# Whole-row query-weight transfers, copied first columns, another order at the layer's end, and the last output-weight rows on eight DMA engines

## The chip, the cores and the metric

The kernel runs on one core of one Trainium2 chip. The metric is the device time of one execution in microseconds (us). The kernel before takes 2003.55 us (median of 4 runs, 2002.02 to 2005.01).

## The reference, cut to what matters

Four attention layers with one query token each run one after the other; layers 0 and 2 share the tensors A, layers 1 and 3 share B. Everything is bfloat16.

```python
D = 640; H = 32; Sk = 8192; Dh = 192             # k_cache, v_cache: (1, 32, 8192, 192); wq (640, 6144); wo (6144, 640)
def attn(x, k_cache, v_cache, wq, wo):
    q = (x @ wq)...                               # 32 heads of 192
    scores = einsum("bhqd,bhkd->bhqk", q, k_cache) * Dh ** -0.5
    p = softmax(scores); o = einsum("bhqk,bhkd->bhqd", p, v_cache)
    return o.reshape(...) @ wo
for W in (A, B, A, B):
    x = x + attn(layernorm(x), *W)
```

A K or V block of one head is 8192 x 192 x 2 bytes = 3072 KB. There are 256 of them in the four layers, six of which the kernel keeps on chip from a layer to the next use. Each is used once against a single query, so nearly all of the time is moving some 849 MB.

## The kernel before

PE is the engine of the matrix products (TensorE), DVE the vector engine, ACT the scalar engine; SP issues the transfers. The kernel has eight slots in SBUF (the on-chip memory of 128 partitions), each big enough for one K or V block. A plan lists all transfers in order; a transfer is issued on one queue (SP) as soon as the slot's last user is done. `m` are a head's products and score matmuls, `s` its softmax, `v` its values, `wq` and `wo` the projections.

```python
# the plan of a layer (cut and shortened)
if l == 0: plan.append(("k", 0, 0)); plan.append(("wq0", 0))
...
elif p < H - 2:  part = [("m", l, p), ("s", l, p), ("v", l, p)]
elif p == H - 2: part = [("m", l, p)]
else:            part = [("m", l, p), ("s", l, p - 1), ("s", l, p), ("v", l, p - 1), ("v", l, p)]
...
if p == H // 2 + 4 and l + 1 < NL: plan.append(("wq0", l + 1))   # next layer's first columns, early
plan.append(("wo", l, 2)); steps.append(("wo", l, 2)); plan.append(("wol", l))

# the transfers (cut and shortened): first two heads' columns of wq, rows of 768 bytes; rest of wq in three pieces of row groups
wq0[:]  <- w["wq"][:, q0:q0 + 2 * DH].rearrange("(p c) n -> p c n", c=5)
t[...]  <- w["wq"][:, q1:q1 + QC].rearrange("(p c) n -> p c n", c=5)[:, c0:c0 + k, :]
# the last two heads' rows of wo (the remainder), 480 KB, behind the third wo part in the same slot
wol     <- w["wo"][wol * DH:(wol + 2) * DH].rearrange("(p i) n -> p i n", p=128)

# a head's products: DVE multiplies K by q in four chunks, PE adds the products up with 24 matmuls
for c in range(4): DV.op(tensor_tensor(k3[:, :, d0:d0 + QD], kin[...], q_sb[...], mult))
for c in range(4): PE.wait(chunks[c]); ... matmul(S, ident, k3[...]) x6
```

Two heads' K blocks come right before their V blocks at the end of a layer: K 30, K 31, V 30, V 31, then the third wo part and the remainder. At the end of layer 1, six of the eight slots hold blocks that are kept, so only two are left to stream through.

## Time and profile before

| what | before | where read |
|---|---|---|
| time | 2003.55 us | median of 4 runs |
| DMA queue's share of 16 engines' span | 99.3% | page, part 3 |
| one K or V block | 7.31 us | distance of landings |
| spread of a block's sixteen landings, start / 1000 us / end | 0.7 / 8.1 / 8.3 us | landings in the trace |
| the stall of layers 1 to 2 | 375 GB/s in its slice | page, part 2 |
| last K, last V fully landed, end of the span | 1973.9, 1988.5, 2002.9 us | landings, page |

Lines of the page of the kernel before: the span, the DMA share in tenths and the GB/s in 40 slices of 50 us, and the DMA queues (q1 carries the kernel's own transfers, q8 and q14 instructions).

```profile
span 2002.9 us, 20412 instructions
...
DMA  9999999999999999999999999999999999999997
GB/s 404 433 430 426 431 430 426 431 431 428 425 431 429 431 429 430 426 432 428 429 375 432 430 429 431 431 427 430 429 429 428 430 428 431 431 429 429 429 431 321
DMA packets 44055, 850.65 MB, mean 425 GB/s; under 512 B 4800, under 2 KB 7360, under 8 KB 7872
...
q1 hardware_dynamic: 43824, 849.37, 99.3%
q8 instruction: 70, 1.15, 0.2%
```

The DMA engines are full nearly always, and the slices say where they are not: the first, the 21st (layer 1 to 2) and the last. Small packets stand out too: 7360 - 4800 = 2560 packets between 512 bytes and 2 KB are the four 768-byte-row transfers.

The timeline of the kernel before at its end (start us, duration us, engine, line, operation, tiles; in brackets the idle time before it and what ended that). L482 are the values' matmuls, L512 the gather of the last heads, L402 the output projection.

```profile
1986.33 2.73 PE L482 MATMUL O<-slot,p_sb 128*2 128x384 bf16 x32
...
1989.75 1.44 PE L512 MATMUL TB<-small,o_sb 128*64 128x1 f32 x12 [0.69 <-ACT o_sb L490]
1991.12 2.73 PE L482 MATMUL O<-slot,p_sb 128*2 128x384 bf16 x32
...
1995.91 3.16 PE L402 MATMUL YB<-oT,slot 128*128 128x1 bf16 x75
```

The last head's values (the second L482 line) have no wait for DMA in brackets: their block had landed at 1988.5, and they queue behind the values and the gather of the head before. The products of that head had started at 1973.93, as its K landed (1973.90).

The same view around the stall of layers 1 to 2, the last product and projection lines:

```profile
999.96 6.76 DVE L433 TENSOR_TENSOR slot<-slot,q_sb 128x3072 bf16<-128x3072 bf16 x4 [0.54 <-DMA slot<-in_B_k_cache_dram]
...
1020.31 3.16 PE L402 MATMUL YB<-oT,slot 128*128 128x1 bf16 x75 [0.22 <-DMA slot<-in_B_wo_dram]
```

Here the projection waits only for wo's landing. The stall starts after that: wq's second piece is asked for when the projection has freed wo's slot, at 1024.1 us.

### The profile page before, as it was taken

How to read it: one execution, taken by the hardware profiler on the slowest of the kernel's cores; microseconds unless marked ns; L12 is line 12 of the kernel's file. 1: busy time of each engine (PE TensorE's matmuls, PEld its weight loads, DVE VectorE, ACT ScalarE, POOL GpSimd, SP SyncE). 2: the span in 40 equal slices, each digit the busy share in tenths (PEclk: the TensorE clock that was granted, in tenths of full speed). 3: DMA queues.
4: the chain of work that ended last, by engine and by line, in shares of the span. 5: the costliest groups of instructions: out<-in, count | busy, mean ns of one | idle time of the engine just before them, and what ended most of it. 6: DMA issues, size and time to landing. Idle time of an engine off the chain costs nothing.

```text
span 2002.9 us, 20412 instructions
## 1 busy us (share of the span) xinstructions
PE 1406.5 (70%) x10438; PEld 323.9 (16%) x7494; DVE 1047.1 (52%) x1072; ACT 217.6 (11%) x657; POOL 4.6 (0%) x22
## 2 busy tenths in 40 slices
PE   5666767667667767767777676676677768767667
PEld 1111111111211111111131111111112212111112
DVE  3454554556345456455535546545564465554554
ACT  0111111111011111111101111111110111111110
POOL 0000000000000000000000000000000000000000
PEclk8788888888688798787878888888886888887887
DMA  9999999999999999999999999999999999999997
GB/s 404 433 430 426 431 430 426 431 431 428 425 431 429 431 429 430 426 432 428 429 375 432 430 429 431 431 427 430 429 429 428 430 428 431 431 429 429 429 431 321
DMA packets 44055, 850.65 MB, mean 425 GB/s; under 512 B 4800, under 2 KB 7360, under 8 KB 7872
## 3 DMA queue, kind: packets, MB, share of 16 engines
q1 hardware_dynamic: 43824, 849.37, 99.3%
q8 instruction: 70, 1.15, 0.2%
q14 instruction: 17, 0.14, 0.0%
q10 hardware_dynamic: 144, 0.00, 0.0%
HBM read 849.35 MB, written 0.00 MB: 424 GB/s over the span
## 4 chain that ended last, share of the span: by engine, by line
DMA 70%; PE 17%; DVE 12%; ACT 1%; issue 1%; another core or an unknown queue 0%; SPq 0%; DVEq 0%
DMA slot<-in_A_k_cache_dram 35%; DMA slot<-in_B_k_cache_dram 34%; PE S L58 11%; DVE slot L433 10%; PE O L482 2%; DMA slot<-in_A_wq_dram 1%; PE S L446 1%; PE TB L497 1%; DVE s_sb L453 1%; ACT p_sb L463 1%; PE TB L467 0%; PE QT L366 0%; DVE small L460 0%; PE YB L402 0%
## 5 line engine op out<-in xcount | busy, mean ns | idle before, releaser
L433 DVE TENSOR_TENSOR slot<-slot,q_sb 128x3072 bf16<-128x3072 bf16 x512 | 865.8, 1753 | 465.3 <-DMA slot<-in_A_k_cache_dram 239.5
L58 PE MATMUL S<-slot,ident 128*128 128x512 bf16 x2944 | 795.6, 424 | 34.1 <-DVE slot L433 34.1
L482 PE MATMUL O<-slot,p_sb 128*2 128x384 bf16 x4096 | 356.8, 428 | 0.0
L446 PE MATMUL S<-slot,ident 128*128 128x512 bf16 x128 | 60.9, 476 | 249.4 <-DVE slot L433 249.2
L453 DVE TENSOR_REDUCE s_sb<-S 128x64 f32<-128x512 f32 x128 | 88.4, 691 | 241.6 <-PE S L58 241.6
L482 PEld LDWEIGHTS O<-slot,p_sb 128*2 128x2 bf16 x4096 | 130.5, 88 | 138.9 <-issue 106.5
L497 PE MATMUL TB<-o_sb,small 128*1 128x192 f32 x480 | 124.0, 391 | 36.3 <-DVE small L471 28.0
L392 ACT ACTIVATE q_sb<-QM 128x192 bf16<-128x192 f32 x120 | 39.7, 331 | 970.7 <-PE QM L385 970.7
L385 PEld LDWEIGHTS QM<-ident,qT 128*128 128x128 bf16 x240 | 23.0, 98 | 731.2 <-issue 715.9
L467 PE MATMUL TB<-small,ones 128*128 128x1 f32 x256 | 50.7, 267 | 109.9 <-ACT p_sb L463 109.9
L457 PE MATMUL QM<-ident,m_bf 128*128 128x128 bf16 x128 | 27.7, 216 | 129.5 <-DVE m_bf L456 129.5
L490 ACT ACTIVATE o_sb<-O,small 128x384 f32<-128x384 f32 x128 | 74.4, 581 | 238.8 <-PE O L482 238.8
L471 DVE RECIPROCAL small<-TB 128x1 f32<-128x1 f32 x128 | 21.5, 168 | 123.3 <-PE TB L467 123.3
L463 ACT ACTIVATE p_sb<-s_sb,small 128x64 bf16<-128x64 f32 x128 | 44.5, 348 | 290.7 <-DVE small L460 290.7
L446 PEld LDWEIGHTS S<-slot,ident 128*128 128x128 bf16 x128 | 12.7, 99 | 331.3 <-DVE slot L433 330.9
L460 DVE TENSOR_REDUCE small<-QM 128x1 f32<-128x128 f32 x128 | 37.3, 291 | 53.2 <-PE QM L457 53.2
L467 PEld LDWEIGHTS TB<-small,ones 128*128 128x128 f32 x256 | 39.9, 196 | 129.6 <-ACT p_sb L463 129.6
L503 ACT ACTIVATE orow<-TB 1x192 bf16<-1x192 f32 x120 | 38.4, 320 | 205.4 <-PE TB L497 205.4
L497 PEld LDWEIGHTS TB<-o_sb,small 128*1 128x1 f32 x480 | 33.5, 89 | 77.7 <-DVE small L471 37.2
L457 PEld LDWEIGHTS QM<-ident,m_bf 128*128 128x128 bf16 x128 | 12.2, 96 | 208.1 <-ACT q_sb L392 131.6
L402 PE MATMUL YB<-oT,slot 128*128 128x1 bf16 x900 | 37.9, 178 | 3.1 <-ACT oT L417 2.2
L402 PEld LDWEIGHTS YB<-oT,slot 128*128 128x128 bf16 x900 | 36.9, 131 | 3.9 <-ACT oT L417 2.9
(47 smaller groups left out, 220.3 us busy)
## 6 DMA issues: line engine op xcount, KB each, us to landing
slot<-in_B_k_cache_dram SPq DMA_DIRECT2D x64, 3072.0 KB, 36.1
slot<-in_A_k_cache_dram SPq DMA_DIRECT2D x63, 3072.0 KB, 23.2
slot<-in_A_v_cache_dram SPq DMA_DIRECT2D x63, 3072.0 KB, 26.3
slot<-in_B_v_cache_dram SPq DMA_DIRECT2D x60, 3072.0 KB, 36.9
slot<-in_A_wo_dram SPq DMA_DIRECT2D x6, 2400.0 KB, 26.3
slot<-in_B_wo_dram SPq DMA_DIRECT2D x6, 2400.0 KB, 34.0
slot<-in_A_wq_dram SPq DMA_DIRECT2D x4, 2880.0 KB, 22.2
slot<-in_B_wq_dram SPq DMA_DIRECT2D x4, 2880.0 KB, 30.7
```

The source lines that it names most:

```text
L58: return t.add_instruction(mybir.InstMatmult(name=t.bass.get_next_instruction_name(), engine=mybir.EngineType.PE, ins=[t.lower_ap(rhs), t. ...
L392: lambda a: a.activation(q_sb[i][:], QM[:, 0:DH], ACT.Copy), e, last["q"][i], bank=use["QM"])
L402: e = PE.op(lambda t, i=i, c=c, f=y_first[0], fin=fin: t.matmul(YB[:, c:c + 1], lhsT=t3[:, i, c:D:DC], rhs=o[:, i:i + 1], start=f, stop=fi ...
L433: e = DV.op(lambda v, d0=d0: v.tensor_tensor(k3[:, :, d0:d0 + QD], kin[:, :, d0:d0 + QD], q_sb[qi][:, d0:d0 + QD].unsqueeze(1).broadcast_t ...
L446: t.matmul(S[:, :], lhsT=ident[:], rhs=k3[:, :, d0:d0 + R], start=True, stop=fin) if d0 == 0 else
L453: ev_s = DV.op(lambda v: v.tensor_reduce(s_sb[par][:], S[:].rearrange("p (j r) -> p j r", r=R), AX.X, ALU.add), ev_S[h], last["s"][par], b ...
L457: e = PE.op(lambda t: t.matmul(QM[:, C_MX:C_MX + P], lhsT=m_bf[par][:, 0:1].broadcast_to([P, P]), rhs=ident[:], start=True, stop=True), ev ...
L463: ev_p[h] = AC.op(lambda a: a.activation(p_sb[par][:], s_sb[par][:], ACT.Exp, bias=negm[par][:, 0:1], accum_out=l_col[par][:]), ev_n, ev_s ...
L467: e = PE.op(lambda t: t.matmul(TB[:, C_L + par:C_L + par + 1], lhsT=ones[:], rhs=l_col[par][:], start=True, stop=True), ev_p[h], last["L"] ...
L482: e = PE.op(lambda e, g=g, j=j, f=m < G, fin=fin: e.matmul(OB[par][32 * g:32 * g + 2, 0:2 * DH], lhsT=p_sb[par][:, j:j + 2], rhs=t[:, j * ...
L490: lambda a: a.activation(o_sb[:], OB[par][:, 0:2 * DH], ACT.Copy, scale=rl[par][:, 0:1]),
L497: e = PE.op(lambda t, i=i: t.matmul(TB[0:1, C_O:C_O + DH], lhsT=pick[:, i:i + 1], rhs=o_sb[:, i * DH:(i + 1) * DH], start=(i == 0), stop=( ...
```

## The change

Its intent: fewer bytes and no small packets (wq of layers 0 and 1 as one transfer of whole rows, 61440 bytes a partition; the first columns that layers 2 and 3 need are copied on chip); a shorter stall (wq's first piece of layer 2 is one row group instead of two, the remainder of wo has its own step and shares the next wq's slot); evened-out DMA engines (the remainder of layers 0 to 2 by eight engines); a shorter tail (another order at the layer's end, and wo's last three row groups as the last transfer). The diff, cut to its core (the two comments after # are added here):

```diff
-    Q_PARTS = [(c, min(2, DC - c)) for c in range(0, DC, 2)]
-    OI = O_LAST * DH // P
+    Q_PARTS = [[(0, 2), (2, 2), (4, 1)] if l < 2 else [(0, 1), (1, 2), (3, 2)] for l in range(NL)]
+    O_PART = [P // 2, P // 2, P // 2, P]
+    OI = [O_LAST * DH // n for n in O_PART]
+    NB = 3
...
-        slot = [sb(f"slot{i}", [P, J * DH], BF16) for i in range(NSLOT)]
+        pool = sb("pool", [P, NSLOT * TS], BF16)          # one tile, so three adjacent slots can hold a whole wq
...
-                    part = [("m", l, p), ("s", l, p - 1), ("s", l, p), ("v", l, p - 1), ("v", l, p)]
+                    part = [("s", l, p - 1), ("m", l, p), ("v", l, p - 1), ("s", l, p), ("v", l, p)]
...
             plan.append(("wol", l))
+            steps.append(("wol", l))
+        plan.append(("wob", NL - 1))
...
+                k = O_PART[l] // O_LAST
+                for h in range(O_LAST):
+                    e = SP.op(lambda s, h=h: s.dma_start(
+                        wol_rows(l)[h * k:(h + 1) * k],
+                        w["wo"][r0 + h * DH:r0 + (h + 1) * DH].rearrange("(q e i) n -> e q (i n)", e=8, i=OI[l])),
+                        *free, sem=semOL, inc=16)
...
+            elif n[0] == "wq" and l < 2:
+                f = lambda s: s.dma_start(pool[:, i * TS:i * TS + DC * QW], w["wq"].rearrange("(p c) n -> p (c n)", c=DC))
...
+                ev_first[l] = DV.op(lambda v: v.tensor_copy(wq0[l][:], whole[:, :, q0:q0 + Q_FIRST * DH]), e)
...
+                for o, i in parts:                          # o_sb of the last two heads, permuted, in two ACT operations
+                    ev_os[h] = AC.op(lambda a, o=o, i=i: a.activation(o, i, ACT.Copy, scale=rl[par][:, 0:1]), ...)
```

## The prediction

> **What bounds it.** The DMA engines. The page gives them 99.3% of the span and 9 tenths or more in nearly every slice; PE has 70%, DVE 52%. A 3072 KB K or V block lands every 7.31 us, all through the kernel. So the time is bytes per engine, plus the places where engines idle, plus the work after the last landing. The trace shows three such places.
>
> 1. *Uneven engines.* A transfer's sixteen landings lie 0.7 us apart at first and 8.1 us at 1000 us, with seven engines ahead and nine some 6 us behind. The instruction queue's 70 packets of 16 KB (about 1.06 us each, durations repeating with period eight) fit a load on half of the engines only. The last engine decides.
> 2. *Layer 1 to 2 (slices of 375 GB/s).* Six of eight slots are kept, and wq's pieces wait for slots: between 1012 and 1050 us the first engines idle about 10 us, the last about 4.
> 3. *The end.* The last product ends at 1982.2, V of the last head lands at 1988.5, but its matmuls start only at 1991.2, behind those of the head before. Then 1.44 us gather, 3.7 us projection (90 matmuls), and some 3 us to the end.
>
> **What changes.**
> - The four transfers of 768-byte rows go (36 ns a packet, 40 an engine: 1.47 us each, read from landings). Two whole-row wq transfers take in their bytes (1.14 us each): 5.9 - 2.3 = 3.6 us less on each engine.
> - Three wo remainders (480 KB) go to eight engines: 2.28 us each on those, none on the others, where it was 1.14 on all. The Trainium skill, "DMA: Bandwidth & Descriptors", "Why a DMA increments its semaphore by 16 and not by 1", says that a transfer uses the largest count of engines up to 16 that divides both sides' slowest dimension, the lowest-numbered ones: here eight. No run shows yet that those are the engines that run ahead; I assume it. Then the late ones end 3.4 us earlier.
> - Layer 2's first wq piece is one row group instead of two, its first heads' columns are already on chip, and wo's slot is released before the remainder. The first K of layer 2 should be asked for about 4 us earlier; idle falls by about 1.6 us (late engines) to 4 us (early ones).
> - At layer ends the softmax and values of head 30 come earlier, so head 31's values can start when V lands: about 2.5 us off the tail. The last three wo row groups arrive last, off the chain.
> - Costs: wq whole, 18.3 us, lands before layer 0 and 1 begin. Four or more blocks are queued behind it, so DMA should not stop. Copies of first columns (1 us of DVE, estimate) are hidden.
>
> **Sum.** Late engines' DMA end: 3.6 + 3.4 + 1.6, about 8.7 us earlier; tail about 2.3 us shorter; together 11 us of 2003.8. Predicted 1992.7 us, range 1989 to 1998. Chances: faster by over 2% 0.01, within 2% 0.97, slower by over 2% 0.02.
>
> **What would show it.** No 768-byte packets; HBM bytes 848.4 MB; spread of landings before the end about 4 us instead of 8.3; the dip at slice 21 smaller but there; chain at the end: head 31's values waiting for DMA, not for PE; last V landing near 1980.
>
> **What would make it wrong.** The eight engines being the late ones (then about 1996 to 1998); a stall at layer 0 to 1, where three adjacent slots must be free at once; long rows delaying instruction fetches or the small x load; whole wq moving slower than 27 GB/s an engine.

## The result, and the profile after

The changed kernel takes 2004.72 us (median of 4 runs: 2003.06, 2002.31, 2006.42, 2006.38); before takes 2003.55 us. The ratio is 1.0005, 95% interval 0.9988 to 1.0022: the same time. Ratios here are the mean time of one kernel's runs over that of the other's runs of the same rounds, so not quite the ratio of the medians quoted beside them.

The page of the changed kernel, the same lines:

```profile
span 2000.9 us, 20649 instructions
...
DMA  9999999999999999999999999999999999999997
GB/s 410 430 430 431 429 429 430 431 431 428 426 431 431 428 430 431 430 430 430 429 380 431 429 428 431 431 428 429 431 428 421 429 430 430 430 428 430 430 430 307
DMA packets 40296, 849.69 MB, mean 425 GB/s; under 512 B 4688, under 2 KB 4688, under 8 KB 5136
...
q1 hardware_dynamic: 40064, 848.38, 99.2%
q8 instruction: 71, 1.16, 0.2%
```

The small packets are gone (4688 under 512 B and as many under 2 KB), and 0.99 MB as well. The traced run is 2.0 us shorter than that of the kernel before, and the last slice is emptier, not fuller: DMA ends earlier, and more time passes after it.

The timeline of the changed kernel at its end. L492 are the products, L58 the score matmuls, L541 the values, L462 the projection.

```profile
1971.99 0.69 DVE L512 TENSOR_REDUCE s_sb<-S 128x64 f32<-128x512 f32 x1 [3.53 <-PE S L58]
...
1974.65 6.75 DVE L492 TENSOR_TENSOR pool<-pool,q_sb 128x3072 bf16<-128x3072 bf16 x4
...
1976.84 7.75 PE L58 MATMUL S<-pool,ident 128*128 128x512 bf16 x23
1984.53 1.47 PE L541 MATMUL O<-pool,p_sb 128*2 128x384 bf16 x32
...
1988.68 2.48 PE L541 MATMUL O<-pool,p_sb 128*2 128x384 bf16 x32
...
1993.58 2.56 PE L462 MATMUL YB<-oT,pool 128*128 128x1 bf16 x60
```

The last K block had fully landed at 1970.52 us, 3.4 us earlier than before. But its products start at 1974.65, 4.1 us after the landing: DVE first has to finish the softmax of head 30, and that waited 3.53 us for the score matmuls of head 30. The values of the last head start 3.6 us after their V block's landing (1985.13), where it had been 2.6. From the last K's landing to the end it is 30.4 us (2000.9 - 1970.5) instead of 29.0.

The landings, taken from the trace's semaphore updates (last engine, in us):

```
                        before     changed
third wo part, layer 0  512.72     509.25
third wo part, layer 1  1020.26    1017.26
second wq piece asked   1024.10    1020.50
first K after stall     1049.96    1046.82
last K                  1973.90    1970.52
last V                  1988.51    1985.13    (predicted: near 1980)
spread at the last V    8.3        7.1        (predicted: about 4)
```

So DMA gains 3.4 us on its late engines instead of the 8.7 predicted, and the tail gives back more than 1 us instead of gaining 2.3. Both errors needed an explanation, and so did the two slow runs of four, 4 us above the others. (A slow run is here one of 2006 us or more.)

### The profile page after: what moved, and what is told of

Read it like the earlier page. It is cut to its first block, busy times and chain, and to the rows that moved or that the text cites. A ratio compares the mean times of both kernels' runs of the same rounds, so it can differ in the third digit from the quotient of the medians.

```text
span 2000.9 us, 20649 instructions
## 1 busy us (share of the span) xinstructions
PE 1404.3 (70%) x10555; PEld 323.1 (16%) x7611; DVE 1049.4 (52%) x1074; ACT 219.8 (11%) x665; POOL 4.5 (0%) x22
## 2 busy tenths in 40 slices
DMA packets 40296, 849.69 MB, mean 425 GB/s; under 512 B 4688, under 2 KB 4688, under 8 KB 5136
## 4 chain that ended last, share of the span: by engine, by line
DMA 67%; PE 20%; DVE 11%; issue 1%; ACT 1%; SPq 0%; another core or an unknown queue 0%; DVEq 0%
DMA pool<-in_A_k_cache_dram 33%; DMA pool<-in_B_k_cache_dram 31%; PE S L58 13%; DVE pool L492 9%; PE O L541 2%; DMA pool<-in_B_wq_dram 1%; DMA x_bf<-in_A_x_dram 1%; DMA pool<-in_B_wo_dram 1%; PE S L505 1%; PE TB L564 1%; PE QT L424 1%; DVE s_sb L512 1%; PE YB L462 1%; ACT p_sb L522 0%; PE TB L526 0%
## 5 line engine op out<-in xcount | busy, mean ns | idle before, releaser
L492 DVE TENSOR_TENSOR pool<-pool,q_sb 128x3072 bf16<-128x3072 bf16 x512 | 865.6, 1753 | 423.4 <-DMA pool<-in_A_k_cache_dram 220.5
L58 PE MATMUL S<-pool,ident 128*128 128x512 bf16 x2944 | 805.5, 428 | 34.7 <-DVE pool L492 34.5
L541 PE MATMUL O<-pool,p_sb 128*2 128x384 bf16 x4096 | 346.7, 417 | 0.0
L505 PE MATMUL S<-pool,ident 128*128 128x512 bf16 x128 | 61.2, 478 | 224.5 <-DVE pool L492 224.5
L541 PEld LDWEIGHTS O<-pool,p_sb 128*2 128x2 bf16 x4096 | 130.4, 87 | 162.0 <-issue 126.2
L556 ACT ACTIVATE o_sb<-O,small 128x384 f32<-128x384 f32 (+1 forms) x136 | 77.4, 581 | 268.0 <-PE O L541 268.0
L505 PEld LDWEIGHTS S<-pool,ident 128*128 128x128 bf16 x128 | 12.7, 99 | 283.7 <-DVE pool L492 282.7
L462 PE MATMUL YB<-oT,pool 128*128 128x1 bf16 x900 | 38.0, 178 | 2.5 <-ACT oT L476 2.2
L462 PEld LDWEIGHTS YB<-oT,pool 128*128 128x128 bf16 x900 | 37.0, 131 | 3.3 <-ACT oT L476 2.9
```

The costliest lines, as they stand in the source:

```text
L58: return t.add_instruction(mybir.InstMatmult(name=t.bass.get_next_instruction_name(), engine=mybir.EngineType.PE, ins=[t.lower_ap(rhs), t. ...
L462: e = PE.op(lambda t, i=i, c=c, f=y_first[0], fin=end and i == k - 1: t.matmul(YB[:, c:c + 1], lhsT=t3[:, i, c:D:DC], rhs=o[:, i:i + 1], s ...
L492: e = DV.op(lambda v, d0=d0: v.tensor_tensor(k3[:, :, d0:d0 + QD], kin[:, :, d0:d0 + QD], q_sb[qi][:, d0:d0 + QD].unsqueeze(1).broadcast_t ...
L505: t.matmul(S[:, :], lhsT=ident[:], rhs=k3[:, :, d0:d0 + R], start=True, stop=fin) if d0 == 0 else
L541: e = PE.op(lambda e, g=g, j=j, f=m < G, fin=fin: e.matmul(OB[par][32 * g:32 * g + 2, 0:2 * DH], lhsT=p_sb[par][:, j:j + 2], rhs=t[:, j * ...
L556: ev_os[h] = AC.op(lambda a, o=o, i=i: a.activation(o, i, ACT.Copy, scale=rl[par][:, 0:1]), e, ev_rl[h], last["osb"], bank=use[f"O{par}"])
```

## The experiments

My theory had two parts. First, the eight lowest-numbered engines are not the early ones, so the eight-engine transfers even out nothing. Second, the softmax of head 30 ahead of the products of head 31 holds those back, at each layer's end. The rivals were the prediction's own steps, and a drawback of the loads that the trace does not show.

### Which engine is late

Sixteen tiny transfers ahead of each remainder, of 1, 2, ... 16 partitions, each with its own semaphore. The Trainium skill, "DMA: Bandwidth & Descriptors", section "Why a DMA increments its semaphore by 16 and not by 1", says that a transfer issued from SP, of n partitions on both sides (n up to 16), uses the n lowest-numbered engines; so the landing that is new in the n-th transfer is that of engine n - 1.

```diff
                 r0 = o["wol"] * DH
+                for q in range(1, 17):
+                    probed[q - 1] = SP.op(lambda s, q=q: s.dma_start(probe[0:q, 8 * (q - 1):8 * q], w["wo"][0:q, 0:8]),
+                                          probed[q - 1], sem=semP[q - 1], inc=16)
```

> The changed kernel with sixteen tiny transfers, of 1, 2, ... 16 partitions, ahead of each wo remainder; the one of n partitions should use the n lowest-numbered engines, so their landings tell how late each numbered engine is. My theory (the eight lowest-numbered engines are half early, half late ones, so the eight-engine transfers balance nothing): of engines 0 to 7 about four are early (0 to 1.5 us behind the earliest) and four late (2 to 5 us behind), and the same of 8 to 15. Rival (the prediction's): 0 to 7 all early. Time within 5 us of the changed kernel.

The time was 2006.35 us (one run, state unknown). The trace shows n engines' landings for the n-th transfer, nested as the skill says (plus one update from the issuing sequencer at once, as that section says too). Each half of an eight-engine remainder shows eight landings and that one update, as the prediction had taken from the same section. How late each engine is behind the earliest, in us:

```
engine           0    1    2    3    4    5    6    7    8    9   10   11   12   13   14   15
end of layer 0  0.3  1.6  0.1  2.4  1.4  3.4  2.9  0.0  0.1  3.4  3.2  3.4  3.2  3.3  3.0  0.0
end of layer 1  3.4  5.1  2.8  7.8  3.9  9.0  8.3  2.2  0.0  5.6  6.7  6.8  5.0  5.1  4.7  0.2
end of layer 2  0.5  1.8  0.0  2.1  0.5  3.3  3.4  0.3  0.6  3.2  3.2  3.0  3.8  3.1  3.4  0.3
end of layer 3  1.9  3.7  1.1  4.9  2.0  8.7  7.1  0.9  0.0  3.6  3.4  3.9  3.8  3.3  4.9  0.4
```

Engines 0, 2, 7, 8, 15 are early, 3, 5, 6 and 9 to 14 late, 1 and 4 between. The first row is from before any eight-engine transfer: engines 0 to 7 are three early, two between, three late. So the assumption is wrong; my expectation of half and half fits the first eight but not the second (two early, six late). After an eight-engine transfer (second and fourth row), engines 5 and 6 are the last, in the second row with 3 close behind: the change has loaded three late engines more. (Before the third row the stall of layers 1 to 2 has closed the gap again: the sixteen landings of a block lie 9.0 us apart before it and 2.0 after it.) A transfer of the lowest-numbered engines can't pick out 0, 2, 7, 8 and 15.

What the remainder on eight engines costs is told by the same kernel with it on sixteen:

```diff
-    O_PART = [P // 2, P // 2, P // 2, P]
+    O_PART = [P] * 4
```

> The changed kernel with the wo remainders of layers 0 to 2 again on 128 partitions and 16 engines. Theory (eight engines are the wrong eight): nothing is lost, the last landing of the last V block stays within 1.2 us of the changed kernel's or comes up to 2 us earlier, spread of landings before the end 7 to 9 us, time within 2 us, rather faster. Rival (the eight engines are the early ones): last V lands 2 to 3.5 us later, spread 9 us or more, time 2 to 3 us slower.

For comparison, the changed kernel was run again on the same chip:

> The changed kernel once more, for runs on the same chip as the others and a second trace. Theory: 0 to 2 us faster than before; last V block landing 3 to 4 us earlier than before, its matmuls starting 3 to 4 us after that landing, as in the first trace. Rival (the equal medians are a drawback that the first trace does not show, for instance a stall in some runs): a median 1 us or more slower than before, or runs in two groups 4 us apart.

The changed kernel took 2007.6 us in these rounds (median of 2002.73, 2007.62, 2007.60, 2004.34, 2008.29; ratio to before 1.0009, 0.9997 to 1.0022). So it has runs some 5 us apart, which the rival had named, and the traced run was the fastest of the five. In that trace the last V landed at 1983.51 and its values started 4.9 us later. With sixteen engines it took 2003.36 us (2002.09 to 2003.91; ratio 0.9994, 0.9982 to 1.0007). The two intervals overlap, but the same step was made at three orders of the layer's end (below), and each time sixteen engines are faster. The edit changes more than the engines, though: the remainder is one transfer instead of two, and PE projects it with 15 matmuls instead of 30. No run separates these. (In the third order, the first K of layer 2 is asked for 13.3 us after wq's second piece with sixteen engines and 15.0 us with eight.) In the trace of the run with sixteen engines the last V landed at 1987.46, later than in the changed kernel's, for another reason: its stall request came late, at 1024.7 us, as in the slow runs further down. Here the expectation (within 1.2 us, or earlier) missed, and this landing alone would have spoken for the rival; the spread was 7.0 us and the time lower, as the theory had it.

### The order at the layer's end

The old order in the changed kernel:

```diff
-                    part = [("s", l, p - 1), ("m", l, p), ("v", l, p - 1), ("s", l, p), ("v", l, p)]
+                    part = [("m", l, p), ("s", l, p - 1), ("s", l, p), ("v", l, p - 1), ("v", l, p)]
```

> The changed kernel with the old order at a layer's end (products of the last head, then softmax of both, then values of both). Theory (softmax of head 30 ahead of the products of head 31 holds those back): the products of head 31 start within 0.1 us of the K landing instead of 4.2 us after, its values start about 17.3 us after the K landing instead of 18.2, and the kernel is 0.5 to 1.5 us faster than the changed one. Rival (the new order shortens the tail, the loss is elsewhere): 1 to 3 us slower than the changed one.

It took 2001.54 us (1998.89 to 2003.08; ratio 0.9987, 0.9973 to 1.0000), about 5 us below the changed kernel in the same rounds by the means (2006.1 and 2001.2). That is more than I expected. Products started at 1970.04 with the K landing at 1970.02, values at 1987.02, 17.0 us after the K.

A third order keeps what the change wanted, the values of head 30 before the softmax of head 31, and lets the products go first:

```diff
+                    part = [("m", l, p), ("s", l, p - 1), ("v", l, p - 1), ("s", l, p), ("v", l, p)]
```

> The changed kernel with the layer end in the order: products of head 31, softmax of 30, values of 30, softmax of 31, values of 31. Theory (products held back by the softmax ahead of them, values of 30 worth having early): products of head 31 within 0.1 us of the K landing, values of head 31 start 14.6 to 16 us after it (18.2 in the changed kernel, 17.1 with the old order), time 1 to 2 us below the old order's, some 0.2% below before. Rival (the order of the softmax does not matter): like the changed kernel.

It took 1999.16 us (1997.78 to 2000.93; ratio 0.9978, 0.9965 to 0.9990). Products started at 1970.62 with the K at 1970.60, and the values of the last head in its timeline start on the landing of V (1985.20), 14.7 us after the K:

```profile
1980.18 1.47 PE L541 MATMUL O<-pool,p_sb 128*2 128x384 bf16 x32
1985.25 1.67 PE L541 MATMUL O<-pool,p_sb 128*2 128x384 bf16 x32 [0.84 <-DMA pool<-in_B_v_cache_dram]
```

Now DMA is named in the brackets: PE waits for data, data does not wait for PE. Its interval and that of the changed kernel in the rounds above (0.9997 to 1.0022) do not meet, so that the order costs time is shown; of the two better orders the intervals overlap.

The same single line was changed in the kernel before:

> The kernel before with nothing changed but the layer end's order (products 31, softmax 30, values 30, softmax 31, values 31). Theory: head 31's values start 0 to 1.5 us after their V block's last landing instead of 2.7, so 1 to 3 us faster than before; that leaves some 4 us of the best version's 6 us to the whole-row wq transfers and copied columns. Rival (the order helps only with the changed loads): under 0.5 us.

It took 2002.84 us against 2004.62 us (ratio 0.9992, 0.9978 to 1.0006). The trace shows what was expected, values at 1987.86 on a landing at 1987.82, and a span 2.0 us shorter; the time is in the expected range, but its interval includes 1, so a gain in the kernel before is not shown.

### Why the changed kernel has slow runs

Two more traces were taken in the hope of a slow run.

> The changed kernel once more, for a trace of one of its slow runs (2006 us or more, some six in ten of the unprofiled ones). Theory (softmax of head 30 ahead of the products of 31 puts PE on the path at the layer ends): in a slow run the first wq piece after the stall of layer 1 to 2 is asked for 2 us or more later than the 1020.4 us of the two fast traces, because the score matmuls of heads 30 and 31 end later. Rival (late engines drift further): that transfer is asked for at 1020 to 1021 us and the last V block lands 3 us later.

> As e10_again_a: the same kernel, another trace, so that one of the two may fall on a slow run of 2006 us or more; the theory expects a late request for wq, the rival a late last V block alone.

Both were slow: 2007.18 and 2006.49 us (single runs, labelled unknown). In both the second wq piece was asked for at 1024.6 and 1024.5 us; in the two fast traces at 1020.5 and 1020.4. That is what the theory expected; the rival had the request in time. From there the 4 us stay to the end (last V at 1989.66 and 1988.65; 1985.13 and 1983.51 in the fast ones). The probe's run (2006.35 us, asked at 1024.3) is a third of this kind, and the run with sixteen engines had the late request too (1024.7), though not the time of a slow run. The timeline of the changed kernel in its first, fast trace:

```profile
1000.63 6.75 DVE L492 TENSOR_TENSOR pool<-pool,q_sb 128x3072 bf16<-128x3072 bf16 x4
...
1002.77 6.70 PE L58 MATMUL S<-pool,ident 128*128 128x512 bf16 x23
...
1017.31 3.16 PE L462 MATMUL YB<-oT,pool 128*128 128x1 bf16 x75 [0.32 <-DMA pool<-in_B_wo_dram]
```

And in the slow trace e10:

```profile
1002.54 6.75 DVE L492 TENSOR_TENSOR pool<-pool,q_sb 128x3072 bf16<-128x3072 bf16 x4
...
1004.73 7.76 PE L58 MATMUL S<-pool,ident 128*128 128x512 bf16 x23
...
1021.46 3.16 PE L462 MATMUL YB<-oT,pool 128*128 128x1 bf16 x75
```

K 31 had landed at 996.93 in the first and 996.86 in the second; the products start 3.7 and 5.7 us after it. In the fast run the projection waits for wo, in the slow one PE itself is late and wo waits (it had landed at 1017.18). The rest goes with the granted clock, the share of its full clock that PE is given at a time; the trace records it. The windows view, length of the window, PE's busy time, granted clock, DMA share and GB/s, of the changed kernel's fast trace:

```profile
1002.00:1012.50 10.50, 8.98 (x59) 0.84 0.94 400
```

Of the slow trace e10:

```profile
1002.00:1012.50 10.50, 8.52 (x30) 0.67 0.94 403
```

And of the third order with sixteen engines (below):

```profile
1002.00:1012.50 10.50, 7.23 (x85) 1.00 0.99 422
```

The clock records of the trace show it in full: in the new order the clock falls to a half at 1002.5 us (fast trace, for 3.4 us) or 1003.2 and 1003.0 us (slow traces, for 6.8 us), after PE has done only three small matmuls in 4.5 us, from the end of head 30's scores to the start of head 31's (997.9 to 1002.4 us in the fast trace). In the kernel before, and in the third order with sixteen engines, it stays full there for 17.1 and 20.5 us. This holds at every layer's end: in all 24 ends of the six traces with the new order the clock is at a half during some of head 31's scores, in none of the 28 of the seven traces with another order. Those scores take 6.7 to 8.2 us in the new order and 5.3 to 6.5 in the others. The case is near the one in the Trainium skill, "TensorE: Matmul & The Clock Gate", section "HAM oscillation — how this bites in real kernels", which warns of idle gaps of more than about 3.4 us on PE, after which the half clock is back; but here PE is not idle throughout, and the longest wholly idle stretch of the gap is 1.9 us.

The second half-clock period comes with a late start: in these 24 ends there was one period in the five where the scores started at most 0.7 us after the drop, and two in the nineteen where they started 1.0 us or more after it. Why, was not tried.

The second period is the smaller part of the 4 us. When the products of head 31 start, the slow trace is already 1.9 us behind (1002.54 against 1000.63): the scores of head 30 ended later, after half-clock spells from 986.2 and 993.0 us that the first fast trace does not have. The scores of head 31 add 1.1 us (8.2 instead of 7.0), and its values 1.0 (2.5 instead of 1.5, at half the clock from 1016.9). The new order passes all this on, because products 31 wait for softmax 30 and so for PE. The third order with eight engines had spells from 986.3 and 993.1 too, and its products still started on the landing of K 31 (998.27 after 998.25).

### The best version

Third order and sixteen engines:

> Both: the middle order and 16 engines. Theory: the lowest of all, 1999 to 2001 us where before has 2004 (ratio 0.997 to 0.9985). Rival: no lower than the changed kernel.

It took 1997.11 us (1996.94 to 1998.11; before 2003.46 in the same rounds; ratio 0.9969, 0.9956 to 0.9981). It beats both kernels, the one before by 0.3%, and is below the 1999 us that I had expected at best, and its runs lie within 1.2 us. Its timeline at the end:

```profile
1968.54 6.77 DVE L492 TENSOR_TENSOR pool<-pool,q_sb 128x3072 bf16<-128x3072 bf16 x4 [0.81 <-DMA pool<-in_B_k_cache_dram]
...
1978.10 1.47 PE L541 MATMUL O<-pool,p_sb 128*2 128x384 bf16 x32
...
1983.16 2.73 PE L541 MATMUL O<-pool,p_sb 128*2 128x384 bf16 x32 [0.83 <-DMA pool<-in_B_v_cache_dram]
...
1987.73 2.56 PE L462 MATMUL YB<-oT,pool 128*128 128x1 bf16 x60
```

Products and values both start on their landings. V landed at 1983.11, 5.4 us earlier than before, and the span ends 11.9 us after it (1995.0).

The last cell of the table, the old order with sixteen engines:

> The old order at the layer's end together with the wo remainders on 16 engines. Theory (late engines 3, 5, 6 no longer get the extra 1.14 us a layer, of which the part since the stall of layer 1 to 2 counts at the end): the last V block's last landing about 1 us earlier than with the old order alone (1984.6), spread 7 to 9 us instead of 10.3, time 0.5 to 1.5 us lower than the old order alone. Rival (eight engines help): 1 to 3 us higher.

It took 2000.88 us (1997.96 to 2001.24; ratio 0.9983, 0.9970 to 0.9995); the last V landed at 1983.58, the spread was 8.0 us. Ratios to before of all six (mean of five runs in us):

| order at the layer's end | remainder on 8 engines | on 16 engines |
|---|---|---|
| softmax 30 ahead of products 31 (the change) | 1.0009 (2006.1) | 0.9994 (2003.1) |
| old order | 0.9987 (2001.2) | 0.9983 (2000.1) |
| products 31, softmax 30, values 30 | 0.9978 (1999.2) | 0.9969 (1997.3) |

The three upper left cells' rounds (the first row and the old order on eight engines) are one set, the other three another, on another chip, so the ratios are the safer comparison. By them (times 2004 us) the order is worth 6.2 us with eight engines and 5.0 us with sixteen, from the first row to the last; sixteen engines are worth 3.0, 0.8 and 1.8 us. The steps across are each close to the width of the intervals or under it; that all three have one sign is what speaks for them. The 3.0 us of the first row is the least clean of them, as three of the five runs on eight engines there are slow ones.

### Whether the bytes were worth what was predicted

The first columns of layers 2 and 3 loaded again as 768-byte rows, not copied, in the kernel with the old order:

```diff
+                if p == H // 2 + 4 and l in (1, 2):
+                    plan.append(("wq0", l + 1))
...
-                ev_first[l] = DV.op(lambda v: v.tensor_copy(wq0[l][:], whole[:, :, q0:q0 + Q_FIRST * DH]), e)
```

> The old order, with the first columns of layers 2 and 3 loaded by transfers of 768-byte rows as in the kernel before, not copied. Theory (the bytes and small packets that the change takes out are worth what was predicted, 1.47 us a transfer on each engine): first and last landings of the last K block 1 to 3 us later than with the old order alone (1959.7 and 1970.0), time 1 to 3 us higher. Rival (small packets cost nothing at the end because idle time at the stall takes it up): under 0.5 us.

It took 2005.20 us (ratio 1.0006, 0.9992 to 1.0020), against 0.9987 for the old order alone: 0.19% or 3.8 us. In the trace, the third wo part of layer 1, after one of the two transfers, lands 1.8 us (first engine) and 2.0 us (last) later, where 1.47 was predicted; the last K lands 4.4 and 4.0 us later, above the 1 to 3 us expected, as is the time. Part of that last figure is not bytes: this trace's stall request came 4.4 us after wo's landing (1018.98 to 1023.39) instead of 3.2 us (1016.98 to 1020.22), at a granted clock of 0.64 against 0.78 between 1012 and 1024 us. Without those 1.2 us it is 2.8 to 3.2 us for two transfers, where 2 x 1.47 = 2.9 was predicted: the step holds, and its size too.

## Why the prediction was wrong

Predicted were 1992.7 us, range 1989 to 1998, 11 us less than before; measured were 2004.72. Point by point:

- *"What bounds it. The DMA engines": right.* In the best version the last V lands 5.4 us earlier, and the values start on that landing.
- *"5.9 - 2.3 = 3.6 us less on each engine": right.* At the end of layer 0, where two of the four small transfers and one taken-in piece count (2 x 1.47 - 1.14 = 1.8 us), the first engine landed 1.9 us earlier (507.60 to 505.72). The last engine landed 3.5 us earlier there, but 2.0 to 3.6 us in the other traces with the changed loads and copied columns, so its landing says less.
- *"No run shows yet that those are the engines that run ahead; I assume it. Then the late ones end 3.4 us earlier": the first step that failed.* The probe shows engines 3, 5 and 6 late. They were given 1.14 us more a layer instead of that much less. The landings, which fall in two groups, told how many engines were late, not which. One cheap run could have told the numbers; the trace before could not. In place of a gain of 3.4 us stands a loss of 1 to 3 us against sixteen engines, by the three pairs of the table (with the other things that this edit changes in it). The prediction named the case and its price ("about 1996 to 1998"), but gave it too little weight, and the range ended there. Even with the right engines three times 1.14 us would hardly all have counted: in the kernel before, the spread falls from 8.1 us at 1012 us to 2.0 at 1055, so the stall of layers 1 to 2 takes up most of what the engines are apart by then. (This is argued from that trace; no run tests it.)
- *"Idle falls by about 1.6 us (late engines)": about right in the best version, lost in the slow runs.* From the last landing of the third wo part to that of the first K after the stall it is 29.7 us before and 28.5 in the best version. In the fast traces of the changed kernel it is 29.6 and 29.2, with 1.14 us more bytes for the late engines 3, 5 and 6 in it; in the two slow traces 33.5 and 33.6. The kernel before in the third order has 28.9, so single traces differ here by nearly as much as the gain. That wq's second piece was asked for at 1020.5 instead of 1024.1 is mostly wo's earlier landing (3.0 us). The stall at layer 0 to 1 that the prediction feared did not come: the slices around 500 us have 428, 426 and 431 GB/s.
- *"The softmax and values of head 30 come earlier, so head 31's values can start when V lands: about 2.5 us off the tail": the second step that failed.* The softmax of head 30 can't start before PE has finished head 30's scores, and DVE took its instructions in the order of the program, so the products of head 31 waited 4.1 us for something that was not theirs. Their scores then took 8.2 us (1976.44 to 1984.60) instead of 6.5, with the clock at a half from 1975.3 to 1982.2. I moved an operation forward without asking what it waits for itself. The tail from the last K on grew by 1.4 us. The goal was right: with the products first, the values do start on V's landing, and from there to the end it is 11.9 us in the best version, where the prediction's 2.3 us off the 14.4 of before make 12.1.
- *A cost that the prediction lacks: PE on the path, and its clock.* In the new order whatever holds PE up in head 30's scores holds up the products of head 31 too, and the gap of some 4.5 us in PE's work before head 31's scores goes with one or two half-clock periods. So the release of wo's slot can come late, and in the stall of layers 1 to 2 nothing hides that: 4 us in both slow runs that were traced. Seven of the eleven timed runs of the changed kernel took 2006 us or more; that the other five had the same cause is likely, not shown.

Without the first failed step the predicted DMA gain is 8.7 - 3.4 = 5.3 us, and in the best version the sum closes, landing by landing of the last engine. It is ahead of the kernel before by 2.8 us at the third wo part of layer 1 (predicted from the bytes up to there: 3 x 1.47 - 2 x 1.14 = 2.1), by 4.0 at the first K after the stall (1.6 more predicted, 1.2 found), and by 5.4 at the last V (1.47 more predicted for the fourth small transfer, 1.4 found). With its tail of 11.9 us instead of 14.4 that makes 7.9 us in the traces, and 6.35 us in the medians of the same rounds. Single traces differ by 1 us and more, so a part of this close fit is luck.

These questions stay open: what a true evening-out of the engines would bring (the early ones can't be addressed by the lowest-numbered rule; the spread in the best version is 8.3 us at the end), why these nine engines are late (the instruction packets are a candidate, but the trace's packets name no engine), how much of the 1 to 3 us of sixteen engines is the engines' own, what the whole-row transfers and the last three row groups of wo are worth alone, and why a late start of the scores goes with a second half-clock period.

## What to carry to other kernels

When landings show that some DMA engines run ahead, find out which with tiny transfers of 1, 2, ... 16 partitions before any load is shifted. Before an operation is moved forward on an engine that takes its instructions in the program's order, ask what that operation itself waits for: whatever stands behind it inherits the wait, and a gap of 4.5 us in TensorE's work went with half the clock here. Where a kernel's runs fall in groups, a trace of a fast run doesn't explain the median: take traces until one is slow.

## What the Trainium skill lacked or had wrong

- "DMA: Bandwidth & Descriptors", section "Latency and other measured facts", has engines 7 and 15 as usually slower in traces (its best guess at the cause holds only for transfers issued from GpSimd). Here, with transfers from SP, they are among the earliest at all four layer ends: engine 15 is 0.0 to 0.4 us behind the earliest, engine 7 is 0.0 to 2.2 us, with the eight-engine transfers' extra load on it in the last three.
- No page says which DMA engines fall behind in a long stream that fills all sixteen. Here 3, 5, 6 and 9 to 14 do, by 2.4 to 3.4 us in the first 500 us, before any uneven load, while 0, 2, 7, 8 and 15 stay within 0.3 us (one trace, of one chip).
- "DMA: Bandwidth & Descriptors", section "Where 436 GB/s comes from", says that for transfers between HBM and SBUF the HBM side binds, at about 358 GB/s; its own table has 425 for one core alone, and it gives 358 as the share when both cores of a pair stream. This one core streams 425 to 433 GB/s in 37 of the 40 slices of the kernel before, so the 358 did not bind here.
